# Rows of the second expert layer turned by VectorE in 32 x 32 blocks, in place of TensorE transposes

## The chip, the cores and the metric

The kernel runs on one core of one Trainium2 chip. The metric is the device time of one execution in microseconds (us). Engines are called as in the profile: PE is TensorE's matmul unit and PEld its weight loads, DVE is VectorE, ACT is ScalarE, POOL is GpSimd, SP is SyncE, which here only issues DMAs.

## What is computed

Three stages over 1536 tokens of 384 features, all in float32. A linear attention with a decaying state gives x. A first layer of 8 experts sends each token to one expert; a second layer sends each token to its two best:

```python
def _moe2_ref(x, w_gate, w_noise, noise, w1, w2):
    logits = x @ w_gate
    noise_scale = np.log1p(np.exp(x @ w_noise))
    noisy_logits = logits + noise_scale * noise
    top2 = np.argpartition(-noisy_logits, 2, axis=1)[:, :2]
    ...
    for e in range(E):
        for k in range(2):
            mask = top2[:, k] == e
            ...
            h = np.maximum(x[mask] @ w1[e], 0.0)
            out[mask] += top2_w[mask, k, None] * (h @ w2[e])
```

E is 8, w1[e] is 384 x 1024 and w2[e] is 1024 x 384.

## The kernel before

Each pair of a layer and an expert is a job: jobs 0 to 7 are the first layer, 8 to 15 the second. The second layer's tokens were written, each with its row of 384 features and 10 further columns (weights, token number, noise), to a table in device memory (`xs2`), sorted by expert, by indirect DMAs from POOL. Its jobs 8 and 9 are experts 0 and 1. The last six, jobs 10 to 15, take the other experts in order of their number of tokens, the fullest first; the expert's number is read into a register on the chip, and the six have room for 432, 412, 400, 396, 384 and 384 tokens (`CAPS`, L28).

A job n has two halves on PE. In the first, eight calls of `hidden(n, f)` (L600) multiply w1 with x, nine matmuls each: every float32 value is split in a high and a low part, and the products high-high, low-high and high-low are added. ACT writes the high part of the result after the ReLU (L613), DVE the low part (L614), from one of three PSUM banks (`ph`). In the second half, eight calls of `second(n, f)` (L619) multiply w2 with these, nine matmuls each (L637). A call of either is called a block below.

Beside this the next jobs are made ready, in an order that the program writes out. `raw(n, i)` (L481) loads a quarter of an expert's weights by a DMA from SP's queue (i = 0, 1 for w1, 2, 3 for w2), into 18 buffers that it shares with the split weights. `split(n, q)` (L496) has ACT write the high part of an eighth of w1 or w2 (L508) and puts the subtraction that gives the low part (L509, on POOL or DVE) on a list, `rest`; `split_rest()` (L511) empties that list after the next block of matmuls.

`load_x(n + 1)` (L542) is called in the first block of job n's first half. It loads the rows of job n + 1 into a buffer of a bank of five (`b6`), from POOL's queue, `nt_` tiles of `p` tokens (4 of 108, or 3 of 128) with the token on the partition. As the matmuls want the feature on the partition, `split_x(n + 1, d)` (L555) turns the features 128 d to 128 d + 127 of all tiles by PE transposes into one of two PSUM banks (`pm`, L567); ACT writes the high part (L571) and DVE the low one (L572) at once. The digits of `XS` (L60) say in front of which blocks of job n's second half the three steps d = 0, 1, 2 stand: "267" for the second layer. The results of a job are turned back, weighted and added to the output in `finish2` (L798), during the next job's first half.

## Time and profile before

| | us |
|---|---|
| median of 3 runs | 494.21 |
| the three runs | 492.13, 494.21, 497.85 |
| the profiled execution | 492.09 |
| its span, from the first to the last instruction | 490.2 |
| PE busy | 474.1 |
| POOL busy | 319.9 |
| DVE busy | 308.4 |
| ACT busy | 262.6 |

The span is that of the one profiled execution, which is 1.9 us shorter than its time. Busy times are unions of the instructions of an engine over the span. Rows of PE give a modelled duration for each matmul, and matmuls overlap, so the step from one start to the next is what one takes of PE's time. The second layer's jobs 9 to 15 run from about 282 us to the end.

### The profile page before, as it was taken

What the parts mean: (1) busy time and instruction counts of PE and PEld (TensorE: products, weight loads), DVE (VectorE), ACT (ScalarE), POOL (GpSimd) and SP (SyncE); (2) the same over time, 40 slices, a digit from 0 to 9 for tenths busy, and PEclk for the clock granted to TensorE, in tenths of its full rate; (3) what the DMA queues carried; (4) which work ended last, traced back from release to release, by engine and by line L of the source; (5) the groups of instructions that cost most, each with busy time, mean ns of one, the idle gap of its engine ahead of it and who ended that gap; (6) DMA issues with size and microseconds to landing.
All of it is one profiled execution on the core that took longest, in us unless ns stands there. A gap on an engine that the chain in (4) does not pass through costs nothing.

```text
span 490.2 us, 9808 instructions
## 1 busy us (share of the span) xinstructions
PE 474.1 (97%) x3542; PEld 445.6 (91%) x3542; DVE 308.4 (63%) x856; ACT 262.6 (54%) x676; POOL 319.9 (65%) x400
## 2 busy tenths in 40 slices
PE   8899999999999999999999999999999999999993
PEld 4588888899999999999998799999999999999993
DVE  7989988557786786786863424735454362746540
ACT  3467787466666675675661356453535536354310
POOL 3434496565777777885865269695794949779322
PEclk9989999999999999999999999999999999999998
DMA  8953863699888868676733854482745847361133
GB/s 284 407 194 137 322 238 103 213 319 283 282 264 264 267 219 274 181 242 216 232 107 105 254 122 151 140 216 78 178 126 156 212 127 165 110 164 21 20 46 42
DMA packets 47797, 91.65 MB, mean 187 GB/s; under 512 B 4625, under 2 KB 29154, under 8 KB 47739
## 3 DMA queue, kind: packets, MB, share of 16 engines
q1 hardware_dynamic: 38090, 70.32, 43.2%
q0 software_dynamic: 9648, 20.61, 18.1%
q8 instruction: 30, 0.49, 0.4%
q14 instruction: 29, 0.23, 0.2%
HBM read 70.63 MB, written 20.28 MB: 185 GB/s over the span
## 4 chain that ended last, share of the span: by engine, by line
PE 68%; DVE 16%; DMA 4%; issue 4%; ACT 4%; POOL 3%; SPq 0%; POOLq 0%; DVEq 0%
PE py L637 28%; PE ph L608 18%; PE ph L611 9%; DMA xs<-b,m_si 3%; PE pm L567 2%; DVE s L509 2%; DVE s L236 2%; DVE h L614 2%; POOL xs L157 2%; PE pm L821 2%; DVE s L253 1%; DVE s L255 1%; PE pm L665 1%; DVE s L240 1%; PE pm L365 1%
## 5 line engine op out<-in xcount | busy, mean ns | idle before, releaser
L509 POOL TENSOR_TENSOR s<-s,s 128x384 fp32r<-128x384 f32 x175 | 184.6, 1263 | 50.1 <-ACT s L508 45.2
L637 PE MATMUL py<-h,s 128*128 128x240 f32 (+5 forms) x1008 | 154.3, 307 | 0.0
L637 PEld LDWEIGHTS py<-h,s 128*128 128x128 f32 x1008 | 142.7, 189 | 1.1
L608 PE MATMUL ph<-x,s 128*128 128x240 f32 (+6 forms) x768 | 136.0, 312 | 1.9 <-DVE h L614 0.9
L508 ACT ACTIVATE s<-s 128x384 fp32r<-128x384 f32 x256 | 123.1, 515 | 1.1 <-DMA s<-w 1.0
L608 PEld LDWEIGHTS ph<-x,s 128*128 128x128 f32 x768 | 115.5, 189 | 4.5 <-DVE h L614 2.5
L614 DVE SCALAR_TENSOR_TENSOR h<-ph,h 128x240 fp32r<-128x240 f32 (+6 forms) x128 | 61.1, 484 | 70.5 <-ACT h L613 63.8
L509 DVE TENSOR_TENSOR s<-s,s 128x384 fp32r<-128x384 f32 x81 | 88.3, 1111 | 3.4 <-ACT s L508 2.7
L613 ACT ACTIVATE h<-ph 128x240 fp32r<-128x240 f32 (+6 forms) x128 | 55.2, 432 | 59.9 <-PE ph L611 55.5
L611 PE MATMUL ph<-x,s 128*128 128x240 f32 (+6 forms) x384 | 76.6, 308 | 0.0
L157 POOL DMA_INDIRECT out<-b,m_ix x29 | 46.5, 1605 | 43.0 <-ACT b L789 23.0
L611 PEld LDWEIGHTS ph<-x,s 128*128 128x128 f32 x384 | 61.2, 189 | 0.4
L571 ACT ACTIVATE x<-pm 128x480 fp32r<-128x480 f32 (+7 forms) x38 | 18.6, 489 | 63.3 <-PE pm L567 63.3
L157 POOL DMA_INDIRECT xs<-b,m_si x32 | 32.9, 1028 | 16.4 <-DVE pm L746 11.4
L298 POOL TENSOR_SCALAR_AFFINE_SELECT h<-h 128x512 f32<-128x512 f32 x24 | 22.1, 942 | 30.8 <-ACT h L297 30.3
L572 DVE TENSOR_TENSOR x<-pm,x 128x480 fp32r<-128x480 f32 (+7 forms) x38 | 20.7, 550 | 27.6 <-ACT x L571 27.2
L637 PE MATMUL py<-s,h 128*128 128x384 f32 x144 | 26.5, 339 | 0.0
L637 PEld LDWEIGHTS py<-s,h 128*128 128x128 f32 x144 | 25.0, 188 | 0.0
L236 DVE TENSOR_TENSOR s<-s,s 112x256 f32<-112x256 f32 (+2 forms) x24 | 19.3, 824 | 1.6 <-DMA s<-qs 1.1
L567 PE MATMUL pm<-iw,b 108*128 108x108 f32 (+5 forms) x129 | 18.7, 260 | 0.8 <-DVE h L865 0.5
L155 POOL MEMSET spacer<- 1x1 f32 x74 | 18.8, 254 | 0.1
L169 PE MATMUL ph<-warm 128*128 128x512 bf16 x66 | 16.9, 415 | 1.5 <-POOL warm L164 1.5
(240 smaller groups left out, 553.9 us busy)
## 6 DMA issues: line engine op xcount, KB each, us to landing
s<-w SPq DMA_DIRECT2D x64, 768.0 KB, 5.7
xs<-s SPq DMA_DIRECT2D x2, 1576.0 KB, 6.5
out<-s SPq DMA_DIRECT2D x4, 768.0 KB, 8.2
b<-xs POOLq DMA_DIRECT2D x4, 664.9 KB
b<-xs POOLq DMA_DIRECT2D x7, 369.4 KB
s<-as SPq DMA_DIRECT2D x2, 780.5 KB
s<-ks SPq DMA_DIRECT2D x2, 768.0 KB, 9.0
s<-qs SPq DMA_DIRECT2D x2, 768.0 KB
```

The costliest lines, as they stand in the source:

```text
L157: st = G.indirect_dma_start(out=dst, out_offset=bass.IndirectOffsetOnAxis(ap=ix, axis=0), in_=src, in_offset=None, **kw)
L236: eng.tensor_tensor(o, src[:, h].rearrange("r (s j) -> r s j", j=64), x[:, h].rearrange("r (s j) -> r s j", j=64), op=ALU.mult)
L298: G.affine_select(a_, a_, pattern=[[0, 4], [1, 128]], compare_op=ALU.is_ge, fill=0.0, base=0, channel_multiplier=-1)
L508: A.activation(hi[sl], t[sl], AF.Copy)
L509: rest.append(lambda: (eng or V).tensor_tensor(lo[sl], t[sl], hi[sl].bitcast(F32), op=ALU.subtract))
L567: PE.transpose(xp[:, k * c + sl.start:k * c + sl.stop], g[:r, t, d * 128:(d + 1) * 128], ident[:r, :r])
L572: V.tensor_tensor(m(xl), xp[:, :w], m(xh).bitcast(F32), op=ALU.subtract)
L608: PE.matmul(p, w, x[:, d, :], start=(k == 0), stop=False)
L611: PE.matmul(p, w1_of(n, f, d)[0], xl[:, d, :], start=False, stop=(d == ND - 1))
L613: A.activation(hh, p, AF.Relu)
L614: V.scalar_tensor_tensor(hl, p, 0.0, hh.bitcast(F32), op0=ALU.max, op1=ALU.subtract)
L637: PE.matmul(out_, l, r, start=(f == 0 and k == 0), stop=(f == NF - 1 and k == 2))
```

## The change

For jobs 10 to 15 the rows come in another form. The ten further columns still come by POOL's queue, one transfer. The 384 features come by four DMAs from SP's queue: the rows are cut in blocks of 32 tokens and their features in four parts of 96; part b goes to partitions 32 b to 32 b + 31, with the token's place in its block on the partition and the blocks side by side. Step d then takes 32 of the 96 columns of every block, and DVE turns all 32 x 32 squares in one instruction into a PSUM bank. A partition so holds another feature than before; the rows of w1 are given to the kernel a second time in that order (`w1_b`), and `raw` loads these for the six jobs. `few_of` lets the code that reads the further columns stay as it is.

The work after the turning is spread: ACT's high part is put on `rest` and so issued after the block of matmuls in front of which the turning stands, DVE's low part after the next block. `split_rest` empties only what is on the list when it is called. The three steps stand in front of blocks 0, 2 and 4 ("024"). The 16 rows behind the 432nd of each of the six experts are set to zero, since blocks of 32 read up to 448 rows.

```diff
-XS = ("467", "267", "677")
+XS = ("467", "024", "677")
...
+            zero_rows(xs2, NF2, E - NF2, C2, -C2 % 32)
...
-            w1, w2 = ap[f"w1_{layer}"][one], ap[f"w2_{layer}"][one]
+            w1, w2 = ap[f"w1_{layer}" if place(n) is None else "w1_b"][one], ap[f"w2_{layer}"][one]
...
         def split_rest():
-            while rest:
-                rest.pop(0)()
+            now, rest[:] = list(rest), []
+            for o in now:
+                o()
...
+        class few_of:
+
+            def __init__(self, x):
+                self.x, self.shape = x, (*x.shape[:2], RW)
+
+            def __getitem__(self, at):
+                p, t, c = at
+                if isinstance(c, slice):
+                    return self.x[p, t, c.start - DM:None if c.stop is None else c.stop - DM]
+                return self.x[p, t, c - DM]
...
-            g = sb([p, nt_, RW], "b6", 5)
             if place(n) is None:
-                rows_ = store[e * R:e * R + nt_ * p]
+                g = sb([p, nt_, RW], "b6", 5)
+                eng.dma_start(g, store[e * R:e * R + nt_ * p].rearrange("(t p) d -> p t d", p=p))
             else:
-                rows_ = store[bass.ds(expert(n, eng.engine) * R, nt_ * p), :]
-            eng.dma_start(g, rows_.rearrange("(t p) d -> p t d", p=p))
+                nb = -(-c // 32)
+                t6 = sb([128, nb * ND * 32 + nt_ * (RW - DM)], "b6", 5)
+                g = few_of(t6[:p, nb * ND * 32:].rearrange("p (t d) -> p t d", t=nt_))
+                eng.dma_start(g[:, :, DM:], store[bass.ds(expert(n, eng.engine) * R, nt_ * p), :].rearrange(
+                    "(t p) d -> p t d", p=p)[:, :, DM:])
+                x = xr_[n] = t6[:, :nb * ND * 32].rearrange("p (t d) -> p t d", t=nb)
+                rows_ = store[bass.ds(expert(n, mybir.EngineType.SP) * R, nb * 32), :]
+                for b in range(4):
+                    nc.sync.dma_start(x[b * 32:b * 32 + 32], rows_.rearrange("(t j) d -> j t d", j=32)[
+                        :, :, b * ND * 32:(b + 1) * ND * 32])
...
+            if place(n) is not None:
+                x = xr_[n][:, :, d * 32:d * 32 + 32]
+                y = pm()[:, :x.shape[1] * 32]
+                V.transpose(y.rearrange("p (t j) -> p t j", j=32), x)
+
+                def high():
+                    A.activation(xh[:, d, :], y[:, :c], AF.Copy)
+                    rest.append(lambda: V.tensor_tensor(xl[:, d, :], y[:, :c], xh[:, d, :].bitcast(F32), op=ALU.subtract))
+
+                rest.append(high)
+                return
...
+    by_block = i["moe2_w1"].reshape(E, 4, ND, 32, F).transpose(0, 2, 1, 3, 4).reshape(E, DM, F)
```

On PE, in job 10's second half, in front of its third block, there stood before (`py` are the results of the second layer of matmuls, `pm` the bank into which x of job 11 is turned, `b` its rows):

```order
L637 MATMUL py_4860<-h_4719,s_845_4546 128x432
L637 MATMUL py_4860<-h_4720,s_845_4546 128x432
L637 MATMUL py_4860<-h_4719,s_846_4547 128x432
L567 MATMUL pm_4879<-iw_83,b_864_4699 128x108 x3
L567 MATMUL pm_4879<-iw_83,b_864_4699 128x88
L637 MATMUL py_4852<-h_4735,s_845_4546 128x432
L637 MATMUL py_4852<-h_4736,s_845_4546 128x432
```

and now, at the same place (L669 is the line of the same matmuls):

```order
L669 MATMUL py_4862<-h_4719,s_846_4554 128x432
L669 MATMUL py_4862<-h_4720,s_846_4554 128x432
L669 MATMUL py_4862<-h_4719,s_847_4555 128x432
L669 MATMUL py_4854<-h_4735,s_846_4554 128x432
L669 MATMUL py_4854<-h_4736,s_846_4554 128x432
```

The four transposes are gone, here and in front of the blocks 6 and 7, and the matmuls of the half follow one another.

On DVE, around the same half, there stood before (the first row is the last hidden low half of job 10, L572 the low parts of x of job 11, L509 low parts of weights, L811 the copy of a result of job 10):

```order
L614 SCALAR_TENSOR_TENSOR h_4847<-ph_4836,h_4846 128x432
L572 TENSOR_TENSOR x_4705<-pm_4879,x_4704 128x412
L509 TENSOR_TENSOR s_903_4866<-s_877_4754,s_902_4865 128x384
L572 TENSOR_TENSOR x_4705<-pm_4937,x_4704 128x412
L572 TENSOR_TENSOR x_4705<-pm_4957,x_4704 128x412
L509 TENSOR_TENSOR s_907_4924<-s_895_4833,s_906_4923 128x384
L811 COPY b_911_4975<-py_4856 128x432
```

and now:

```order
L646 SCALAR_TENSOR_TENSOR h_4847<-ph_4836,h_4846 128x432
L584 STREAM_TRANSPOSE pm_4852<-b_864_4695 128x416
L588 TENSOR_TENSOR x_4705<-pm_4852,x_4704 128x412
L584 STREAM_TRANSPOSE pm_4883<-b_864_4695 128x416
L588 TENSOR_TENSOR x_4705<-pm_4883,x_4704 128x412
L584 STREAM_TRANSPOSE pm_4914<-b_864_4695 128x416
L510 TENSOR_TENSOR s_904_4869<-s_877_4754,s_903_4868 128x384
L588 TENSOR_TENSOR x_4705<-pm_4914,x_4704 128x412
L510 TENSOR_TENSOR s_909_4928<-s_895_4833,s_908_4927 128x384
L843 COPY b_911_4966<-py_4858 128x432
```

Three turnings came in, behind job 10's last hidden low half and each ahead of its subtraction, and two of the three subtractions of x now stand ahead of the weights' first one.

## Rows read from the trace of the kernel before

**Rows 1.** The page: busy time of PE, and the chain that ended last.

```profile
PE 474.1 (97%) x3542; PEld 445.6 (91%) x3542; DVE 308.4 (63%) x856; ACT 262.6 (54%) x676; POOL 319.9 (65%) x400
...
PE 68%; DVE 16%; DMA 4%; issue 4%; ACT 4%; POOL 3%; SPq 0%; POOLq 0%; DVEq 0%
PE py L637 28%; PE ph L608 18%; PE ph L611 9%; DMA xs<-b,m_si 3%; PE pm L567 2%; DVE s L509 2%; DVE s L236 2%; DVE h L614 2%; POOL xs L157 2%; PE pm L821 2%; DVE s L253 1%; DVE s L255 1%; PE pm L665 1%; DVE s L240 1%; PE pm L365 1%
```

**Rows 2.** Busy us by stage: 9's second half, 10's and 11's first, 14's second.

```profile
core 0: us, PE busy (x) PEld busy (x) DVE busy (x) ACT busy (x) POOL busy (x), PEclk, DMA share, GB/s
296.50:311.80 15.30, 15.30 (x86) 14.60 (x86) 10.54 (x6) 8.34 (x19) 14.25 (x16) 1.00 0.30 101
311.80:327.30 15.50, 15.50 (x86) 14.69 (x85) 6.04 (x14) 8.20 (x17) 11.92 (x16) 1.00 0.87 229
...
342.60:357.40 14.80, 14.80 (x86) 14.56 (x85) 5.86 (x13) 8.08 (x17) 11.33 (x15) 1.00 0.75 182
...
442.90:456.50 13.60, 13.60 (x83) 13.51 (x82) 9.21 (x9) 5.68 (x13) 10.59 (x13) 1.00 0.07 9
```

**Rows 3.** L567 from 297 to 460 us: ns min/median/max, first and last start.

```profile
L567 PE MATMUL pm<-iw,b x66: 227/256/273, 300.0 to 454.7; 108*128 108x108 f32 x39, 128*128 128x128 f32 x18, 88*128 88x88 f32 x3, 76*128 76x76 f32 x3
```

**Rows 4.** PE in order of time, job 9's second half: start us, us, what.

```profile
296.52 3.69 PE L637 MATMUL py<-h,s 128*128 128x432 f32 x18
300.04 0.53 PE L567 MATMUL pm<-iw,b 108*128 108x108 f32 x4
300.35 7.29 PE L637 MATMUL py<-h,s 128*128 128x432 f32 x36
...
311.77 1.34 PE L608 MATMUL ph<-x,s 128*128 128x432 f32 x6
```

**Rows 5.** PE in order of time, job 14's second half.

```profile
442.85 3.28 PE L637 MATMUL py<-s,h 128*128 128x384 f32 x18
445.97 0.49 PE L567 MATMUL pm<-iw,b 128*128 128x128 f32 x3
446.22 6.53 PE L637 MATMUL py<-s,h 128*128 128x384 f32 x36
...
456.40 1.21 PE L608 MATMUL ph<-x,s 128*128 128x384 f32 x6
```

**Rows 6.** Groups of DVE from 297 to 457 us: busy us, mean ns, idle before.

```profile
L509 DVE TENSOR_TENSOR s<-s,s 128x384 fp32r<-128x384 f32 x13 | 40.0, 3083 | 2.0 <-ACT s L508 1.3 <-POOL s L509 0.7
...
L572 DVE TENSOR_TENSOR x<-pm,x 128x432 fp32r<-128x432 f32 x3 | 1.7, 598 | 3.3 <-ACT x L571 3.3
```

**Rows 7.** SP's queue 297 to 480 us (packets, MB, share); loads, us to landing.

```profile
q1 hardware_dynamic: 9189, 15.54, 27.1%
...
s<-w SPq DMA_DIRECT2D x64, 768.0 KB, 5.7
...
out<-s SPq DMA_DIRECT2D x4, 768.0 KB, 8.2
```

**Rows 8.** SP's DMA issues in order of time.

```profile
83.48 0.85 SPq L200 DMA_DIRECT2D xs<-s  x2
97.01 0.36 SPq L591 DMA_DIRECT2D b<-xs  x1
...
272.70 7.74 SPq L493 DMA_DIRECT2D s<-w  x2
...
311.20 1.00 SPq L493 DMA_DIRECT2D s<-w  x2
```

**Rows 9.** ACT in order of time, at the start of job 9.

```profile
282.72 0.56 ACT L789 ACTIVATE b<-pm,b 88x384 f32<-88x384 f32 x1
```

**Rows 10.** POOL in order of time, ends of jobs 10 and 14, [idle before].

```profile
341.95 1.01 POOL L509 TENSOR_TENSOR s<-s,s 128x384 fp32r<-128x384 f32 x1 [5.75 <-ACT s L508]
...
455.99 1.01 POOL L509 TENSOR_TENSOR s<-s,s 128x384 fp32r<-128x384 f32 x1 [3.01 <-ACT s L508]
```

**Rows 11.** DVE in order of time: last lows of job 10, first of 11.

```profile
327.63 1.63 DVE L614 SCALAR_TENSOR_TENSOR h<-ph,h 128x432 fp32r<-128x432 f32 x3
...
345.00 0.59 DVE L614 SCALAR_TENSOR_TENSOR h<-ph,h 128x412 fp32r<-128x412 f32 x1 [0.43 <-ACT h L613]
```

More of the change, by code (lines that the diff above doesn't have):

```diff
@@ L196, in body, with zero_rows @@
         zt = []
-        def zero_rows(store, e, n, r):
-            nc.sync.dma_start(store[:E * R].rearrange("(e r) d -> r e d", e=E)[r:r + 128, e:e + n],
-                              zt[0][:, None, :RW].to_broadcast([128, n, RW]))
+        def zero_rows(store, e, n, r, k=128):
+            nc.sync.dma_start(store[:E * R].rearrange("(e r) d -> r e d", e=E)[r:r + k, e:e + n],
+                              zt[0][:k, None, :RW].to_broadcast([k, n, RW]))
         def zero_xs1():
@@ L522, in w2_of @@
             return hi[:, f % 4, :], lo[:, f % 4, :]
-        xg, xsp = {}, {}
+        xg, xsp, xr_ = {}, {}, {}
+        class few_of:
[6 more added lines that the diff above has]
+                return self.x[p, t, c - DM]
         def dims(n):
@@ L1362, in prepare @@
         "wgn": i["moe_w_gate"],
-        "w1_1": i["moe_w1"], "w2_1": i["moe_w2"], "w1_2": i["moe2_w1"], "w2_2": i["moe2_w2"],
+        "w1_1": i["moe_w1"], "w2_1": i["moe_w2"], "w1_2": i["moe2_w1"], "w1_b": by_block, "w2_2": i["moe2_w2"],
     }
```

## Prediction

> **What bounds the kernel now.** I read the page's summary first, then busy time by stage, then PE in order of time, and last the queues of SP, DVE and POOL. PE is busy for 474.1 of 490.2 us and carries 68% of the chain that ended last; its largest two lines are both matmuls of the experts [rows 1]. In the second layer there is no gap at all: in the four halves of jobs shown, of twelve alike, 13.6 to 15.5 us long, PE is busy from end to end at granted clock 1.00, that is at the 2.4 GHz level, while DVE is busy for 5.9 to 10.5 us and POOL for 10.6 to 14.3 us [rows 2]. So an instruction taken off PE there is worth its whole place in PE's row, for as long as nothing else becomes late. What counts is PE's step from start to start, not the duration in a row: the four transposes of a group last 256 ns each in the middle [rows 3], yet the group starts at 300.04 us and the next matmul at 300.35 us [rows 4], so they cost 78 ns apiece.
>
> **What the change removes from PE.** 66 transposes in 18 groups: three groups for each of six jobs (of 4 tiles for x of jobs 10 to 13, of 3 tiles for x of jobs 14 and 15) [rows 3]. There are two ways to price them.
> - By their slots: 0.31 us for a group of four [rows 4], 446.22 − 445.97 = 0.25 us for a group of three [rows 5]; 12 × 0.31 + 6 × 0.25 = 5.2 us.
> - By what the whole second half would take without them. In that of job 9, 18 matmuls run undisturbed from 296.52 to 300.04 us, 0.1956 us each, so 72 take 14.08 us; the half lasts until 311.77 us, 15.25 us, which is 1.17 us more [rows 4]. In that of job 14, 18 take 3.12 us, 72 take 12.48 us, and the half lasts 456.40 − 442.85 = 13.55 us: 1.07 us more [rows 5]. The four jobs between give 1.03 to 1.25 us in the same way, all six 6.83 us.
>
> The second is larger because the matmuls just behind a group also start some 0.08 us late. That goes with the group, so I take 6.8 us as the gain, and 5.2 us as its lower bound.
>
> **What it adds.** 18 block transposes on DVE, of 384 to 448 columns each, from the bank's tile in SBUF to PSUM. No row of this kernel shows one. The nearest is the subtraction for x, which streams 432 columns from PSUM and SBUF in 598 ns; the farthest is the subtraction for the weights, both of whose inputs lie in SBUF, and which takes 3083 ns in this stretch [rows 6]. I take 0.6 us, since a transpose streams one operand, and keep 3.1 us for the range: 11 us of DVE in all, or 55 us. What hides it: DVE is free for 4.4 us and more of each half shown [rows 2], against 1.8 us that three transposes take, and PE waits for DVE only at two points, the low half of x before the next job's first nine matmuls end, and the hidden low halves that free the three PSUM banks of the first layer of matmuls. The order of DVE shows each transpose right before the subtraction that goes with it, behind the last hidden low half of the job, so nothing that the running job's second half reads stands behind a transpose. Three steps at blocks 0, 2 and 4 leave three blocks, over 5 us, until the next job starts; ACT's conversion and DVE's subtraction are as many as before and of the same size. If that cover went, each block of delay would show as a wait on PE at the start of a job.
>
> **What it moves.** The rows of x leave POOL's queue for SP's: four transfers a job of 32 partitions with 384 B pieces, 12 to 14 per partition, so 1536 to 1792 pieces a job. The hardware queue's 9189 packets here took 27.1% of 16 engines over 183 us, 86 ns each; 1792 of them are at most 9.6 us of all engines (at 86 ns), at least 2.2 us (688 KB at the same bytes per second) [rows 7]. In a job of some 29 us, with the engines up to 87% busy in one half and less in the other [rows 2], that fits. On SP the four stand between the loads of w1 and of w2 of the same expert. SP runs ahead of PE: the w2 loads of job 11 are issued at 311.20 us, about when job 10 starts, and they are used from job 10's second half on, at 327 us [rows 2, 8]. For jobs 11 to 15 the rows of x thus start more than 20 us before they are turned. Job 10's is the tight one: its bank can be held until ACT has weighted the last tile of job 8, at 283.3 us [rows 9], where the w2 loads behind it were issued at 272.70 us [rows 8]; so they come some 11 us later, and x is wanted at 296.5 us. 13 us for transfers whose neighbours of like size land in 5.7 us [rows 7] is enough, so I cost this at nothing. POOL keeps a load of ten columns a row with as many pieces, so its time stays. The added zeroing of 96 rows goes out at about 84 us on SP, whose next load leaves at 97 us [rows 8]: nothing. The weights in a second order of rows are read with the same shapes: nothing. The changed emptying of the list of delayed subtractions changes nothing where no entry adds another.
>
> **The sum.** The profiled execution took 492.09 us for a span of 490.2 us; less 6.8 us that is 485.3 us. The median of the three runs shown, 494.21 us, stands 2.1 us above it, so I predict 494.2 − 6.8 = 487.4 us, 1.4% less.
>
> **The rivals.**
> 1. *Only the slots go* (5.2 us): 489.0 us, if the late starts behind a group come from the change of bank rather than from the group. Against it: in jobs' halves without groups the step stays even.
> 2. *Another engine's row is as long as PE's*, so that what PE saves turns into waits: 494 us. For it: POOL is busy for up to 14.3 of 15.3 us [rows 2]. Against it: POOL waits for ACT at the end of each job, 5.75 us at job 10 and still 3.01 us at job 14 [rows 10], and PE gives up only 1.1 to 1.2 us a job.
> 3. *x of job 10 lands late*, because its four transfers run one after another at 8.2 us each, the longest landing in [rows 7]: 283.3 + 33 = 316 us, and about 3 us more through DVE and ACT. Job 10 would start at 319 us instead of 310.6 us, and ACT, stuck at a split of the w2 rows behind, would hold it some 2 us more: 494.2 − 6.8 + 11 = 498 us. Against it: SP's loads overlap one another.
> 4. *The transposes cost DVE 3.1 us each* because POOL holds them up as it does the weights' subtractions [rows 6]. At job 10, DVE ends its hidden low halves at 329.3 us and starts those of job 11 at 345.0 us [rows 11]; three transposes at 3.1 us with their conversions and subtractions, and the weights' two, would end 3 to 5.5 us later. PE's fourth block of job 11 needs the bank that the first of them frees, and would wait 1.2 to 3.8 us, say 2.5 us a job: 494.2 − 6.8 + 15 = 502 us. It decides from about 2.7 us a transpose on. For it: the 3083 ns. Against it: DVE's operations with one operand in PSUM stay near 0.6 us in the same stretch, with POOL as busy. The Trainium skill (SBUF — State Buffer, section "SBUF: two separate sides") says that GpSimd locks VectorE out only where VectorE's operation has two SBUF inputs or runs in a two-port mode. The trace agrees for the two kinds that it shows; a transpose has one SBUF input, so by that rule this rival falls.
> 5. *Each transpose is worth its own duration*, 66 × 0.256 = 16.9 us [rows 3]: 477.3 us. The Trainium skill (TensorE: Matmul & The Clock Gate, section "Part 4: PE-mode transpose") gives some 275 ns for a transpose in one kernel's context, by which the gain would be an estimated 18.2 us. The rows' durations agree with that figure, but the starts 78 ns apart [rows 4] show that most of it overlaps.
>
> That the transposes go from PE and come on DVE is settled by the order; the features' new places on the partitions are matched by the rows of the weights.
>
> **How the numbers follow.** Forecast 0.67 (485 to 489 us); rival 1 0.08, rival 2 0.10, rival 3 0.06, rival 4 0.07, rival 5 0.02. About 1% is what a measurement of this kernel can tell from no change (the three runs lie between 492.13 and 497.85 us). Faster by over 1%, below 489.3 us: nearly all of the forecast, half of rival 1, rival 5: 0.69. Slower by over 1%: rival 4 and a part of rival 3: 0.09. Within 1%: the rest, 0.22. The range goes from 484.5 us to rival 2's 494.0 us, which holds the forecast and rivals 1 and 2.
>
> **What would show it.** Right: second halves of 14.1 us (job 9) to 12.5 us (job 14) with 72 matmuls on end, PE without waits in the second layer, DVE's transposes at about 0.6 us, the seam waits of POOL about 1 us shorter. Wrong: a wait of PE at a job's start on DVE's x or on its hidden low halves (rivals 3, 4), transposes of 2 us and more, a step between matmuls that is longer than 0.196 us at 432 columns, or SP holding w2 loads past their use.

## The result, and the profile after

| | before | after |
|---|---|---|
| median, us | 493.17 (4 runs) | 487.53 (4 runs) |
| profiled execution, us | 492.09 | 485.4 |
| its span, us | 490.2 | 483.8 |

The ratio is 0.9904, 95% interval 0.9877 to 0.9931: 5.6 us or 1.0% less, where 6.8 us or 1.4% was forecast. Two later rounds with the same kernel gave 0.9908 (0.9877 to 0.9939) and 0.9913 (0.9885 to 0.9941).

The page after, for [rows 1]:

```profile
PE 466.5 (96%) x3473; PEld 438.6 (91%) x3476; DVE 306.4 (63%) x874; ACT 262.5 (54%) x676; POOL 322.0 (67%) x400
...
PE 76%; DVE 10%; issue 5%; ACT 4%; POOL 2%; DMA 1%; SPq 0%; DVEq 0%; POOLq 0%
```

PE is still the bound, and carries more of the chain than before. PE in order of time, job 9's second half and the start of job 10, for [rows 4]:

```profile
294.67 14.23 PE L669 MATMUL py<-h,s 128*128 128x432 f32 x72
308.75 1.34 PE L640 MATMUL ph<-x,s 128*128 128x432 f32 x6
309.92 0.75 PE L643 MATMUL ph<-x,s 128*128 128x432 f32 x3
311.03 0.81 PE L853 MATMUL pm<-iw,b 128*108 128x128 f32 x3 [0.36 <-ACT b L845]
311.59 1.42 PE L640 MATMUL ph<-x,s 128*128 128x432 f32 x6
```

The half is one row of 72 matmuls, and takes 308.75 − 294.67 = 14.08 us, to the hundredth what the forecast named. The rows behind it are not as forecast. The same place in the kernel before:

```profile
312.95 0.75 PE L611 MATMUL ph<-x,s 128*128 128x432 f32 x3
313.53 0.49 PE L821 MATMUL pm<-iw,b 128*108 128x128 f32 x3
313.78 1.42 PE L608 MATMUL ph<-x,s 128*128 128x432 f32 x6
```

From the last three matmuls of job 10's first block to the next matmul it was 0.58 us and is now 1.11 us, with a wait for ACT; the three transposes of job 9's results behind it (L821, now L853) held PE for 0.25 us and now hold it for 0.56 us.

Busy time by stage, for [rows 2]; job 9's second half, job 10's first and second, job 14's second:

```profile
core 0: us, PE busy (x) PEld busy (x) DVE busy (x) ACT busy (x) POOL busy (x), PEclk, DMA share, GB/s
294.70:308.80 14.10, 14.10 (x74) 13.56 (x73) 11.17 (x8) 6.04 (x14) 12.64 (x14) 1.00 0.74 198
308.80:325.10 16.30, 15.88 (x86) 14.59 (x85) 7.37 (x14) 10.26 (x23) 13.73 (x16) 1.00 0.60 143
325.10:339.20 14.10, 14.10 (x73) 13.54 (x72) 7.68 (x13) 6.32 (x14) 11.61 (x13) 1.00 0.79 191
448.80:461.50 12.70, 12.70 (x74) 12.70 (x73) 5.02 (x13) 4.39 (x9) 5.07 (x7) 1.00 0.37 47
```

Of these four, only job 10's first half has PE below its full time. POOL's wait for ACT at the end of each job, 5.75 us at job 10 and 3.01 us at job 14 [rows 10], is not 1 us shorter but gone: the subtraction that waited there now stands in POOL's row before it, which has ten where it had nine. Laid side by side by the starts of the halves, the two profiles give this (sums of our own, from PE in order of time):

| us | before | after | difference |
|---|---|---|---|
| up to job 9's start | 282.24 | 280.39 | −1.85 |
| second halves of jobs 9 to 14, sum | 86.99 | 80.45 | −6.54 |
| first half of job 10 | 15.50 | 16.33 | +0.83 |
| the other first halves, 9 and 11 to 15 | 84.23 | 84.35 | +0.12 |
| job 15's second half | 13.05 | 13.05 | 0 |
| from PE's end to the span's end | 8.19 | 9.23 | +1.04 |
| span | 490.2 | 483.8 | −6.4 |

The first line is not the change's: in three profiles of the changed kernel job 9 starts at 280.39, 279.15 and 281.40 us. The change's own terms are −6.54, +0.83, +0.12 and +1.04, together −4.55 us, as the two later ratios have it (0.9908 × 489.4 is 4.5 us less, 0.9913 × 489.2 is 4.3).

DVE's groups from 294 to 462 us, for [rows 6] (busy us, mean ns, idle before), and below them the range of the turnings (ns min/median/max):

```profile
L510 DVE TENSOR_TENSOR s<-s,s 128x384 fp32r<-128x384 f32 x13 | 29.4, 2263 | 1.4 <-ACT s L509 0.7 <-POOL s L510 0.7
...
L584 DVE STREAM_TRANSPOSE pm<-b 128x416 f32<-128x416 f32 x9 | 5.6, 617 | 0.0
```

```profile
L584 DVE STREAM_TRANSPOSE pm<-b x18: 582/616/651, 296.0 to 442.4; 128x416 f32<-128x416 f32 x9, 128x384 f32<-128x384 f32 x6, 128x448 f32<-128x448 f32 x3
```

A turning takes 0.62 us in the middle, as taken (0.6), and never near the 3.1 us of the other end. SP's queue from 297 to 475 us, for [rows 7], and its issues in order of time, for [rows 8]:

```profile
q1 hardware_dynamic: 17385, 18.26, 35.6%
...
b<-xs SPq DMA_DIRECT2D x12, 156.0 KB, 3.3
```

```profile
267.63 3.68 SPq L571 DMA_DIRECT2D b<-xs  x4
271.56 7.05 SPq L494 DMA_DIRECT2D s<-w  x2
...
301.61 1.94 SPq L571 DMA_DIRECT2D b<-xs  x4
```

The queue's packets are nearly twice as many (17385, where 9189 were), and the block loads land in 3.3 us in the median. Job 10's rows were not held back to 283.3 us; they left at 267.63 us. What they did do is stand in front of the w2 loads.

**Where the 0.83 us of job 10 comes from.** POOL, DVE and ACT of the changed kernel in order of time, [idle before <- what ended it]:

```profile
281.26 1.59 POOL L157 DMA_INDIRECT out<-h,m_ix  x1 [9.00 <-ACT h L821]
...
287.31 1.60 POOL L157 DMA_INDIRECT out<-b,m_ix  x1 [4.43 <-DVE h L646]
...
289.54 17.81 POOL L510 TENSOR_TENSOR s<-s,s 128x384 fp32r<-128x384 f32 x18
```

```profile
297.73 0.65 DVE L584 STREAM_TRANSPOSE pm<-b 128x448 f32<-128x448 f32 x1
299.28 0.61 DVE L588 TENSOR_TENSOR x<-pm,x 128x432 fp32r<-128x432 f32 x1 [0.90 <-ACT x L587]
300.57 7.20 DVE L510 TENSOR_TENSOR s<-s,s 128x384 fp32r<-128x384 f32 x1 [0.68 <-POOL s L510]
307.69 0.65 DVE L584 STREAM_TRANSPOSE pm<-b 128x448 f32<-128x448 f32 x1
308.25 0.53 DVE L510 TENSOR_TENSOR s<-s,s 128x384 fp32r<-128x384 f32 x1
```

```profile
308.37 0.53 ACT L587 ACTIVATE x<-pm 128x432 fp32r<-128x432 f32 x1 [7.48 <-DVE pm L584]
308.80 1.75 ACT L509 ACTIVATE s<-s 128x384 fp32r<-128x384 f32 x4
310.46 0.94 ACT L845 ACTIVATE b<-py 128x432 f32<-128x432 f32 x2
```

To be read backwards. PE waits for the copies of job 9's results, two by ACT (L845) and one by DVE (L843). ACT makes its two only at 310.46 us, behind its high part of x, for which it stood still 7.48 us, and four conversions of weights. It stood still for the third turning, and that stood behind one subtraction of weights on DVE. The next such subtraction takes 0.53 us at 308.25, but this one, which starts at 300.57 inside POOL's unbroken row of 18 subtractions, takes 7.20 us; it ends 0.4 us after that row does (289.54 + 17.81 = 307.35). POOL's row begins behind the scatter of 287.31 us (L157; called POOL's third scatter below, and that of 281.26 us the second), 6.05 us after the scatter before; in the kernel before the two stood 5.12 us apart (283.11 and 288.23 us). The kernel before held DVE up in the same way:

```profile
302.47 8.59 DVE L509 TENSOR_TENSOR s<-s,s 128x384 fp32r<-128x384 f32 x2 [0.69 <-POOL s L509]
```

But there PE made the third turning, and only near the half's end, and ACT's copies stood behind nothing late.

### The profile page after: what moved, and what is told of

Read it like the earlier page. It is cut to its first block, busy times and chain, and to the rows that moved or that the text cites. A ratio compares the mean times of both kernels' runs of the same rounds, so it can differ in the third digit from the quotient of the medians.

```text
span 483.8 us, 9795 instructions
## 1 busy us (share of the span) xinstructions
PE 466.5 (96%) x3473; PEld 438.6 (91%) x3476; DVE 306.4 (63%) x874; ACT 262.5 (54%) x676; POOL 322.0 (67%) x400
## 4 chain that ended last, share of the span: by engine, by line
PE 76%; DVE 10%; issue 5%; ACT 4%; POOL 2%; DMA 1%; SPq 0%; DVEq 0%; POOLq 0%
PE py L669 30%; PE ph L640 20%; PE ph L643 10%; DVE h L646 2%; PE ph L290 2%; PE pm L366 2%; DVE s L510 2%; ACT s L509 2%; PE pm L853 2%; PE pm L697 1%; PE py L337 1%; PE py L343 1%; PE py L317 1%; PE pm L599 1%; ACT h L645 1%
## 5 line engine op out<-in xcount | busy, mean ns | idle before, releaser
L669 PE MATMUL py<-h,s 128*128 128x240 f32 (+5 forms) x1008 | 150.6, 306 | 0.0
L669 PEld LDWEIGHTS py<-h,s 128*128 128x128 f32 x1008 | 143.7, 189 | 1.2
L509 ACT ACTIVATE s<-s 128x384 fp32r<-128x384 f32 x256 | 123.1, 515 | 0.9 <-DMA s<-w 0.9
L157 POOL DMA_INDIRECT out<-b,m_ix x29 | 46.5, 1604 | 56.1 <-ACT b L821 33.9
L510 DVE TENSOR_TENSOR s<-s,s 128x384 fp32r<-128x384 f32 x81 | 77.3, 975 | 2.8 <-ACT s L509 2.1
L157 POOL DMA_INDIRECT xs<-b,m_si x32 | 32.9, 1028 | 16.5 <-DVE pm L778 11.4
L299 POOL TENSOR_SCALAR_AFFINE_SELECT h<-h 128x512 f32<-128x512 f32 x24 | 23.3, 991 | 27.1 <-ACT h L298 26.5
L669 PE MATMUL py<-s,h 128*128 128x384 f32 x144 | 25.9, 338 | 0.0
L669 PEld LDWEIGHTS py<-s,h 128*128 128x128 f32 x144 | 25.2, 188 | 0.0
L587 ACT ACTIVATE x<-pm 128x384 fp32r<-128x384 f32 (+4 forms) x18 | 9.1, 506 | 22.6 <-DVE pm L584 22.6
L845 ACT ACTIVATE b<-py 128x432 f32<-128x432 f32 (+4 forms) x12 | 5.9, 501 | 27.0 <-PE py L669 27.0
L603 ACT ACTIVATE x<-pm 128x480 fp32r<-128x480 f32 (+3 forms) x20 | 9.5, 473 | 17.6 <-PE pm L599 17.6
```

Of the source, the lines that this page charges most:

```text
L157: st = G.indirect_dma_start(out=dst, out_offset=bass.IndirectOffsetOnAxis(ap=ix, axis=0), in_=src, in_offset=None, **kw)
L299: G.affine_select(a_, a_, pattern=[[0, 4], [1, 128]], compare_op=ALU.is_ge, fill=0.0, base=0, channel_multiplier=-1)
L509: A.activation(hi[sl], t[sl], AF.Copy)
L510: rest.append(lambda: (eng or V).tensor_tensor(lo[sl], t[sl], hi[sl].bitcast(F32), op=ALU.subtract))
L669: PE.matmul(out_, l, r, start=(f == 0 and k == 0), stop=(f == NF - 1 and k == 2))
```

## The experiments

The last two columns of this table will be used below: from the second to the third scatter of POOL in job 9 (L157), and from PE's end to the span's end. "Firsts" and "seconds" are sums over jobs 9 to 15 and 9 to 14. All but the medians and ratios are from one profile each, good to about 0.05 us.

| kernel | median, us | ratio (95%) | job 10's first | firsts | seconds | scatters | end |
|---|---|---|---|---|---|---|---|
| before | | 1 | 15.50 | 99.73 | 86.99 | 5.12 | 8.19 |
| after | 487.53 | 0.9904 (0.9877–0.9931) | 16.33 | 100.68 | 80.45 | 6.05 | 9.23 |
| change_again | 484.58 | 0.9908 (0.9877–0.9939) | 16.09 | 100.45 | 80.43 | 5.79 | 9.42 |
| change_third | 485.22 | 0.9913 (0.9885–0.9941) | 16.35 | 100.70 | 80.43 | 6.00 | 9.52 |
| steps023 | 484.70 | 0.9911 (0.9894–0.9928) | 17.64 | 102.01 | 80.42 | 6.60 | 9.56 |
| steps246 | 485.60 | 0.9930 (0.9916–0.9945) | 17.77 | 101.98 | 80.37 | 6.55 | 9.70 |
| order_only | 490.30 | 1.0022 (1.0010–1.0035) | 15.80 | 102.11 | 85.33 | 5.09 | 8.33 |
| turn_thrice | 484.57 | 0.9906 (0.9885–0.9926) | 18.34 | 102.67 | 80.31 | 6.67 | 8.10 |
| turn_six | 515.68 | 1.0511 (1.0485–1.0537) | 21.55 | 134.27 | 80.27 | 7.36 | 9.49 |
| loads_as_before | 482.58 | 0.9854 (0.9830–0.9878) | 15.53 | 99.83 | 80.37 | 5.10 | 8.44 |
| pool_all | 482.48 | 0.9858 (0.9833–0.9884) | 15.51 | 99.71 | 80.43 | 6.15 | 8.14 |
| pool_all_again | 482.43 | 0.9865 (0.9840–0.9890) | 15.50 | 99.67 | 80.46 | 6.10 | 8.06 |
| loads_and_pool | 482.43 | 0.9855 (0.9834–0.9876) | 15.52 | 99.81 | 80.38 | 5.10 | 8.14 |
| last_three | 488.20 | 0.9980 (0.9965–0.9996) | 15.80 | 101.66 | 83.06 | 5.21 | 9.15 |

The kernel before had medians of 493.17 us beside the first result, and 489.46 us (steps023, order_only, steps246, turn_thrice), 489.38 us (pool_all, loads_as_before, turn_six, change_again) and 489.20 us (the rest) beside the others.

**1. The third turning one block earlier.** If the turning is late because it stands behind the subtraction, it should be made ahead of it.

```diff
-XS = ("467", "024", "677")
+XS = ("467", "023", "677")
```

> The changed kernel with the third step one block earlier (in front of blocks 0, 2, 3). Theory A (in the changed kernel the third turning of job 10's x stands on DVE behind a weights' subtraction that waits 7.2 us while POOL works, ACT waits behind it, and job 10's first half becomes 0.8 us longer): the third turning now stands ahead of that subtraction, starts by 301 us of the changed kernel's time instead of 307.7, job 10's first half falls from 16.3 to about 15.5 us, and the time is about 0.8 us under the changed kernel's, 5.5 to 6.5 us under the kernel before. Theory B (the longer half comes from PE's earlier start alone, as the weighting of job 9 has to wait for PE's copies either way): the half stays at 16.3 us and the time at that of the changed kernel, 4.7 us under the kernel before.

The turning did go ahead, to 299.07 us, and yet job 10 lost more, 2.14 us over the 15.50 before. DVE in order of time:

```profile
299.07 0.65 DVE L584 STREAM_TRANSPOSE pm<-b 128x448 f32<-128x448 f32 x1
...
300.84 10.56 DVE L510 TENSOR_TENSOR s<-s,s 128x384 fp32r<-128x384 f32 x3
311.32 0.60 DVE L843 COPY b<-py 128x432 f32<-128x432 f32 x1
```

Now the three subtractions stood together, held up until POOL's row ended, and the copy of a result behind them: PE waited 1.93 us for that copy (L843). So the turning was only one of the things that stand behind the held-up subtraction, and the subtraction itself is the suspect; number 6 tests it. The 1.3 us that this profile has in job 10 over the change's do not show in the medians (484.70 us is 4.8 us below the kernel before, as the change is in its second round).

**2. The same order with PE's transposes.** The kernel before, with nothing but the places of the steps changed.

```diff
-XS = ("467", "267", "677")
+XS = ("467", "024", "677")
```

> The kernel before, with its PE transposes, but with the three steps in front of blocks 0, 2, 4. Theory A (the gain is PE's places): no gain, within 0.5 us of the kernel before, second halves still 15.3 to 13.5 us, only the places of the transposes in them move. Theory B (the gain comes from x being ready earlier than the end of the half): 2 us or more of the change's 4.7 us are here, with first halves shorter than before.

No gain, and 0.2% lost. The halves of jobs 9 to 15, without the last, add up to 187.44 us against 186.72: each group costs as much at its new place, and the first of job 10's waits 0.3 us for its rows. The gain lies in the transposes that are gone.

**3. All three turnings one or two blocks later.**

```diff
-XS = ("467", "024", "677")
+XS = ("467", "246", "677")
```

> The changed kernel with the steps as late as the three-step order allows, in front of blocks 2, 4, 6. Theory A (three blocks of slack are more than needed): the low part of the last third of x is issued after the half's last block, DVE and ACT run ahead of PE there, so PE waits at no job's start, second halves stay at 14.1 to 12.6 us, time within 0.7 us of the changed kernel. Theory B (the early steps are needed to hide the longer way through DVE and ACT): PE waits 0.5 to 1.5 us at the start of each of six jobs for x, 3 to 9 us in all, and most of the gain is gone.

The second halves are as short, job 10's first half is 2.27 us longer than before, and PE waits at its start for the high part of x (1.11 us). By job 10's first half, in one profile each, "024" is better than its neighbours on either side, but none of the three is free of POOL's row. The timing tells neither neighbour from it: the interval of 0.9930 overlaps with all three of the change.

**4. Each turning three times.** The bound on DVE's spare time: two more turnings of the same data behind each, so 36 more of 0.6 us.

```diff
-                V.transpose(y.rearrange("p (t j) -> p t j", j=32), x)
+                for _ in range(3):
+                    V.transpose(y.rearrange("p (t j) -> p t j", j=32), x)
```

> The changed kernel with each turning on DVE done three times over, which adds 36 transposes of 0.58 to 0.65 us, 22 us of DVE. Theory A (DVE has 4.4 us and more free in each second half, and PE waits for it nowhere): time within 1 us of the changed kernel, no new wait of PE at the start of jobs 11 to 15; if anything job 10, where DVE is already late, loses up to 1 us more. Theory B (DVE is close to being the bound once PE is shorter): each job loses what its DVE is longer, 3.7 us, up to 22 us in all; between them a loss of 1 us a job.

Some 22 us more of DVE leave the ratio that of the change. That is not all cover: in the profile job 10 pays 2.0 us more than in the change, where DVE is short, and the end is 1.1 us shorter, of which below, so the two nearly cancel. Jobs 11 to 15 pay nothing (firsts within 0.06 us of the change's). For these five the cover that the forecast named for 0.6 us holds up to 1.9 us a step; for job 10 it does not hold at 0.6 us.

**5. Each turning six times.** The same edit with `range(6)`; 3.9 us a step, past the 2.7 us from which rival 4 was to decide.

> The changed kernel with each turning done six times over, 3.5 to 3.9 us a step, which is over the 3.1 us of rival 4 of the prediction. Theory A (rival 4's working): at 3.7 us a step DVE ends the last hidden low halves' successors some 5 to 8 us late, PE waits 3 to 6 us at the start of each job, and the time is 15 to 30 us over the changed kernel's. Theory B (DVE runs ahead of PE in the second half, as it waits for nothing that PE makes there, so that three steps of 3.7 us still fit before the next job): jobs 11 to 15 lose under 1 us each; only job 10, where POOL holds DVE up, loses 3 to 5 us.

26 us slower than before, with a loss in each of the six jobs. DVE, PE and the waits of PE around the start of job 11:

```profile
344.29 3.92 DVE L585 STREAM_TRANSPOSE pm<-b 128x416 f32<-128x416 f32 x6
```

```profile
345.92 0.91 PE L641 MATMUL ph<-x,s 128*128 128x412 f32 x4
348.81 0.64 PE L641 MATMUL ph<-x,s 128*128 128x412 f32 x2 [1.98 <-ACT x L588]
...
351.62 2.41 PE L641 MATMUL ph<-x,s 128*128 128x412 f32 x6
```

```profile
352.00:358.00 6.00, 6.00 (x26) 5.81 (x26) 2.08 (x6) 2.43 (x5) 4.79 (x7) 0.65 0.26 30
```

The first halves of jobs 10 to 15 are 33.6 us longer than in the change. The waits themselves are 16.8 us for x in six times and 2.6 us for the results' copies. The rest goes with the clock: after a wait the granted clock of the next 6 us is 0.65 in the mean, between the levels of 2.4 and 1.2 GHz, and six matmuls of a block that last 1.28 to 1.38 us in the change last 2.41 us. The six first halves have granted clocks of 0.92, 0.84, 0.91, 0.85, 0.84 and 1.00 in the mean, where the change has 1.00 in all; by these shares of their lengths that is an estimated 13.4 us, and 33.6 − 16.8 − 2.6 = 14.2 us were left to explain. The wait came in the job's first block, on x, not in its fourth on a bank of PSUM.

**6. POOL takes all low parts of job 9's time.** If DVE's subtraction is what is held up, then POOL, which holds it up, should make it.

```diff
-            eng = [G if x == "G" else V for x in ENGS[layer - 1]]
+            eng = [G if x == "G" or n == E + 1 else V for x in ENGS[layer - 1]]
```

> The changed kernel with all low parts of weights that are split during job 9 put on POOL (in the second half four of twelve stood on DVE). Theory A (what job 10's first half loses in the changed kernel comes from DVE's subtractions with both inputs in SBUF, which don't end before POOL's unbroken run does, and hold DVE's turning, ACT behind it and the copies of job 9's result): DVE turns all of x by 303 us, PE waits nowhere at job 10's start, its first half takes 15.5 us instead of 16.3, POOL's run grows by four subtractions of 0.985 us and ends near 313 us, which nobody waits for; time 0.8 us or more under the changed kernel's, 5.5 to 6.5 us under the kernel before. Theory B (POOL's row is the bound at job 9): the longer run makes job 10 later by up to 4 us, and the time is 2 to 4 us over the changed kernel's.

0.9858, 1.4% less than before: job 10's first half is back at 15.51 us, and PE has no wait there. DVE of this kernel:

```profile
300.18 0.65 DVE L584 STREAM_TRANSPOSE pm<-b 128x448 f32<-128x448 f32 x1
301.73 0.61 DVE L588 TENSOR_TENSOR x<-pm,x 128x432 fp32r<-128x432 f32 x1 [0.90 <-ACT x L587]
308.74 0.61 DVE L843 COPY b<-py 128x432 f32<-128x432 f32 x1 [6.40 <-PE py L669]
309.26 4.37 DVE L798 TENSOR_SCALAR m_iz<-b 108x4 f32<-108x4 f32 x1
```

```profile
290.00 23.59 POOL L510 TENSOR_TENSOR s<-s,s 128x384 fp32r<-128x384 f32 x24
```

POOL's row is now 24 long and ends 5.9 us later after job 9's start than in the change, and POOL's third scatter is as late as in the change (6.15 us): neither matters to PE. DVE makes all three turnings without delay, and the copies come on time.

**7. The rows by one load from POOL, turned by DVE all the same.** This takes the four block loads of each job out of SP's queue; where the rows fill only 108 partitions, one load of weights (L568) fills the other 20, in the block loads' place in that queue. What is turned is not the right rows, so the output of jobs 10 to 15 is not the reference's; the instructions on PE, DVE and ACT are those of the change.

```diff
-                eng.dma_start(g[:, :, DM:], store[bass.ds(expert(n, eng.engine) * R, nt_ * p), :].rearrange(
-                    "(t p) d -> p t d", p=p)[:, :, DM:])
+                eng.dma_start(g, store[bass.ds(expert(n, eng.engine) * R, nt_ * p), :].rearrange("(t p) d -> p t d", p=p))
...
-                for b in range(4):
-                    nc.sync.dma_start(x[b * 32:b * 32 + 32], rows_.rearrange("(t j) d -> j t d", j=32)[
-                        :, :, b * ND * 32:(b + 1) * ND * 32])
+                if p < 128:
+                    nc.sync.dma_start(t6[p:, :nb * ND * 32], ap["w1_2"][0].rearrange("d f -> (d f)")[
+                        :(128 - p) * nb * ND * 32].rearrange("(p w) -> p w", p=128 - p))
...
```

> DVE turns as in the changed kernel, but the rows come as before, in one load from POOL's queue of all columns, and no blocks come by SP (20 partitions that this leaves empty are filled from weights, so what is turned isn't x of the tokens: the output of jobs 10 to 15 is not the reference's). Theory A (the new loads cost nothing): time within 1 us of the changed kernel, second halves equal to 0.1 us. Theory B (the four transfers of 384 B pieces hold up SP's loads of weights or the scatters): the time is 1 to 3 us under the changed kernel's.

0.9854. The third scatter comes 5.10 us after the second, as in the kernel before, POOL's row ends sooner (26.0 us after job 9's start, where it was 27.0), and job 10's first half is 15.53 us, though DVE is still held up:

```profile
287.03 1.60 POOL L157 DMA_INDIRECT out<-b,m_ix  x1 [3.48 <-DVE h L644]
...
289.25 17.80 POOL L510 TENSOR_TENSOR s<-s,s 128x384 fp32r<-128x384 f32 x18
```

The new loads do cost something: the kernel is 2.0 us below the change beside it (482.58 and 484.58): 0.6 us are job 10's first half, 0.9 to 1.0 us the end of the program, of which below.

So the block loads are what makes the scatter late. Of all profiles, those with block loads in front of job 10's w2 loads have 5.79 to 7.36 us between the scatters, those without 5.09 to 5.21. The traces show how. The second scatter's own packets (the software queue) start to move 3.0 to 3.2 us after job 9's start in all fourteen. In the five without block loads SP's queue (the hardware queue) has by then been empty for about 1 us, since its last packet ended 1.7 to 2.1 us after job 9's start; in the nine with them it goes on to 4.5 to 6.5 us, side by side with the scatter's packets, whose last one starts 5.5 to 7.0 us after job 9's start and not 4.8 to 4.9. The third scatter starts 1.17 to 1.20 us behind that in all fourteen. The queues from 3 to 5 us after job 9's start, first in the kernel before, then in the changed one (packets, MB, share of the 16 engines):

```profile
q0 software_dynamic: 144, 0.20, 81.0%
```

```profile
q0 software_dynamic: 135, 0.19, 70.2%
q1 hardware_dynamic: 80, 0.11, 15.2%
```

Whether it is the block loads' own bytes or the w2 load behind them that makes SP's queue run on is not separated. The first w2 load leaves 8.83 us before job 9's start, where it left 9.54 us before it, but this lateness does not set the delay: in change_again it is the larger (8.18 us) with the scatters 5.79 us apart, in pool_all the smaller (9.23 us) with 6.15 us.

**8. Both repairs together, and the change and the first repair beside them.** loads_and_pool has the edits of 6 and 7; pool_all_again and change_third are those kernels once more.

> Both single repairs together: VectorE turns, but rows come by one POOL load as before (so the output of jobs 10 to 15 is not the reference's), and POOL takes all low parts of the split during job 9. My theory (one mechanism: the block loads make POOL's run start about 0.9 us later, and VectorE's subtraction, which cannot end before that run ends, is then late for job 10; either repair ends it): no gain over either alone, first half of job 10 at 15.5, POOL's third scatter 5.1 us after the one before it, ratio 0.9855 within 0.002. Rival (moved loads and the locked VectorE are two separate costs of 0.8 us): ratio 0.984 or below, job 10's first half under 15.0.

> The changed kernel with POOL taking all low parts of the split during job 9, a second time, beside the changed kernel on the same chip. My theory: 0.8 to 1.0 us under the changed kernel's median, first half of job 10 at 15.5, no wait of TensorE over 0.3 us in jobs 9 to 15; ratio 0.986. Rival (its lead in the earlier call was only scatter between runs): the medians within 0.3 us of each other.

> The changed kernel itself beside the two repairs. My theory: ratio 0.9905, first half of job 10 between 16.1 and 16.4, POOL's third scatter 5.8 to 6.1 us after the one before it. Rival (job 10's loss is a chance of single profiles): first half of job 10 at 15.5 with POOL's run still late.

Together they bring no more than either alone (0.9855, 0.9865): the late scatter and the held-up subtraction are one mechanism, not two costs. The repair leads the change by 2.8 us here (482.43 and 485.22) and by 2.1 us in the earlier round (482.48 and 484.58). The intervals of their ratios just overlap in either round, but both rounds agree. That is more than the 0.6 to 0.85 us of job 10; most of the rest stands, with 1.3 to 1.5 us, in the table's last column, in the end of the program.

**9. The change itself a second time**, beside 5 to 7.

> The changed kernel itself, as the measure of the other three on the same chip: ratio to the kernel before 0.990 to 0.991, second halves 14.1 to 12.6 us, job 10's first half 16.3 us or longer by up to 1 us, as DVE's and POOL's order of events there varies.

Job 10's first half 16.09 us with the scatters 5.79 us apart; all the rest as in the first profile.

**10. Only the last three jobs turned.** Jobs 10 to 12 keep PE's transposes and POOL's loads.

```diff
+        def turned(n):
+            return place(n) is not None and place(n) >= 3
...
-            w1, w2 = ap[f"w1_{layer}" if place(n) is None else "w1_b"][one], ap[f"w2_{layer}"][one]
+            w1, w2 = ap["w1_b" if turned(n) else f"w1_{layer}"][one], ap[f"w2_{layer}"][one]
...
-            if place(n) is not None:
+            if turned(n):
```

> Only jobs 13 to 15 of the second layer's six blocks of rows are turned by VectorE; jobs 10 to 12 are loaded and turned by TensorE as before. My theory (each turned job gives back what its four slots cost in the second half of the job before, and the seam at job 10 is lost only where the block loads of job 10 make POOL's run late): second halves of jobs 12, 13 and 14 as in the changed kernel (13.12, 12.96, 12.63), those of jobs 9 to 11 as before (15.25, 15.29, 14.64), job 10's first half back at 15.5, and the sum of these three gains 3.1 us: ratio 0.9937 to the kernel before. Rival (the first turned job pays about 0.8 us wherever it stands): job 13's first half 15.1 instead of 14.3, ratio 0.995. Rival (the gain comes from the bank or the queue freed for good, not slot by slot): the halves before job 12 move too.

The second halves of jobs 12 to 14 are 13.12, 12.96 and 12.64 us, those of the change, and no first half from job 12 on lost more than 0.06 us: slot by slot, as I had it. The ratio is not as I had it, since I had forgotten that "024" stays: job 9 waits for job 10's rows in front of its first block (PE, in order of time), and its two halves last 0.89 us longer than before together. With the long end (9.15) that eats up 1.85 of the 3.1 us; 1.2 us remain, and 1.0 were measured.

```profile
295.52 0.56 PE L605 MATMUL pm<-iw,b 108*128 108x108 f32 x4 [0.70 <-DMA b<-xs]
```

**The end of the program.** From PE's end on, the last copy and scatter come at the same distances (the last scatter starts 0.90 us later before and after, in change_third and in pool_all_again). Then the scatter's data land, and the program ends. In seven profiles (before, order_only, turn_thrice, both of pool_all, loads_as_before, loads_and_pool) PE's end is 8.06 to 8.44 us before the span's end, in the other seven 9.15 to 9.70 us. In each of these seven the trace shows one transfer of the queue of instructions that starts 2.0 to 2.2 us before the end, when no other transfer is going on, and in none of the first seven is there one from 2.8 to 0.2 us before the end. The DMA queues of the changed kernel from 480 us on:

```profile
DMA packets 1, 0.01 MB, mean 2 GB/s; under 512 B 0, under 2 KB 0, under 8 KB 0
...
q14 instruction: 1, 0.01, 0.7%
```

Whether a piece of program is fetched there seems to hang on how many instructions each engine has, not on what they do: turn_thrice is the change with 36 more instructions on DVE, and has the short end; turn_six, with 90 more, has the long one; pool_all only moves a few subtractions from DVE to POOL, and has the short one. Which engine's count it is stays open. The Trainium skill (Runtime: NRT & Kernel Launch, section "Instruction fetch mechanics") says that an engine's program is fetched block by block while it runs, and that crossing from one block to the next is mostly hidden; here it comes when no other transfer is going on, and the seven ends are 1.2 us longer in the mean. No run moved the fetch by itself, so that the fetch costs the 1.2 us is not shown; it rests on the fourteen profiles going together.

## Why the prediction was right, and where not

- **The time itself: partly luck.** 487.53 us came out where 487.4 us was forecast, but the forecast counted from 494.2 us, and the kernel before stands at 493.17 us in the comparison and at 489.2 to 489.5 us in the later ones. The change is worth 5.6 us in that comparison and 4.8 and 4.0 us in the later two, not 6.8 us; the direction and the main term were right, and what was missed (below) takes a third of the forecast gain in the profile.
- **The gain on PE** (6.83 us by whole halves): 6.54 us in the profile, and 6.5 to 6.7 in every kernel that turns all six. The price by halves was the right one; rival 1's price by slots (5.2) falls, and so does rival 5's (16.9). The transposes' late successors belonged to the groups and went with them.
- **The turning on DVE** (0.6 us, range to 3.1): 0.62 us, inside POOL's rows too. Rival 4's premise, that POOL holds them up, falls; the rule of the Trainium skill that spoke against it (SBUF — State Buffer, section "SBUF: two separate sides") agrees with the trace: 582 to 651 ns with one input in SBUF, beside the 7.20 us of the subtraction with two. Its turning point, 2.7 us a step, lies where the runs leave it for jobs 11 to 15, between 1.9 and 3.9 us; its place and price were wrong: 31 us over the change at 3.9 us a step, where I had 15 at 3.1, and at the first block, a part of it through the clock.
- **"PE waits for DVE only at two points", and "nothing that the running job's second half reads stands behind a transpose."** This step failed. The second sentence is true of that half, but it looked only at what is read inside it, and the list of two points lacks a third: the copies of the half's results, which PE turns back in the next half. They stand on ACT behind the high part of x, and on DVE behind the weights' subtraction, which did not end before POOL's row did. The cover (three blocks, 5 us, and 4.4 us of free DVE) took DVE's other work as short; DVE was busy 11.17 of 14.10 us there, 7.20 us of it in one held-up subtraction. Price 0.83 us, once. It is not rival 2, in which POOL's row itself is too long: in pool_all that row ends 5.9 us later, and PE waits nowhere.
- **The loads moved to SP, costed at nothing.** Their landing was no problem, as said (3.3 us), and rival 3 falls: job 10's rows left at 267.63 us. What I left out is what else is moving when the queue runs on: it was still busy when a scatter of POOL moved its data, the scatter landed late, and that made POOL's row late enough to matter (experiments 7 and 8).
- **The end of the program, not in the sum at all:** +1.04 us in the profile, 1.2 us in the mean.
- **The sum.** −6.8 forecast; −6.54 + 0.95 + 1.04 = −4.55 us in the profile's terms, −4.0 to −5.6 us by the medians of three comparisons. Without job 10's loss and with the short end, the kernel does what was forecast: pool_all is 6.9 and 6.8 us below the kernel before (489.38 − 482.48, 489.20 − 482.43).

## What to carry to other kernels

When work is moved to an engine, look not only at what waits for the moved work, but at all that stands behind it in that engine's and the next engine's order, the results' way out included. An engine's busy time is no spare time turned round: here DVE's long rows were one short subtraction waiting for POOL's row to end, and giving that subtraction to POOL, the busier engine, was worth more than either of the other places tried for the new work. A transfer put in a queue is priced also by what else is moving when the queue now ends.

## What the runs showed of the hardware that was not expected

- A DVE subtraction with both inputs in SBUF, 0.53 us alone, was not served between two of POOL's subtractions for as long as these followed each other without a seam: it waited for the end of the row (7.20 us after, 6.23 us in loads_as_before, the first of three in steps023 likewise; each ended 0.42 to 0.43 us after the row). In that row each of POOL's subtractions starts 0.26 to 0.3 us before the one before it ends, one every 0.98 us. In rows with a seam, where one starts only as the one before it ends, DVE is let in. The changed kernel has such a row from 325.70 to 336.68 us, with a seam at 333.11 us; DVE's subtraction there takes 1.61 us and ends at 333.53 us, 3.15 us ahead of the row's end:

```profile
331.92 1.61 DVE L510 TENSOR_TENSOR s<-s,s 128x384 fp32r<-128x384 f32 x1
```

  Over all fourteen profiles, 334 of these DVE subtractions start while one of POOL's is running; 302 of them end within 0.06 us of 0.42 us after the next seam of POOL's row (an overlap under 0.1 us), the other 32 up to 1.3 us sooner or 1.9 us later.

  The Trainium skill (SBUF — State Buffer, section "SBUF: two separate sides") says that the pair of ports is locked for one whole instruction. The trace agrees that DVE stands still; it shows besides that the wait can last over many instructions of POOL where they overlap.
- Small operations of DVE from SBUF to SBUF are held up as well: 108 x 4 elements took 4.37 us in pool_all, until POOL's row ended (309.26 + 4.37 = 313.63, 290.00 + 23.59 = 313.59).
- One fetch of program near the end, when the last data have landed, goes with 1.2 us of the time, a quarter of what this change gained in its profile.
